# A fused attention and two-layer-pair kernel: GpSimd left out of the last two stages, operands loaded earlier

## The chip, the core and the metric

The kernel runs on one core of a Trainium2 chip, all of it in one launch. The metric is the time of one execution on the device in microseconds. The core's engines that matter here are TensorE (PE in the rows; its weight loads are PEld), VectorE (DVE), ScalarE (ACT), GpSimd (POOL) and SyncE (SP), which issues all DMA transfers of this kernel. Each works through its own instructions in order and waits for the others by semaphores.

## What is computed

Attention (local and coarse) over 4 x 8 heads of 576 tokens gives x of 2304 tokens by 512; two products, a gate, and two more products follow. Then comes the part that the change touches:

```python
def _moe_ref(x, w1, w2, w3, w_out):
    a = x @ w1
    b = x @ w2
    h = a * b @ w3
    return (h @ w_out).astype(np.float32)

def _moe2_ref(x, w_in, w_out):            # x: 2304 x 512, w_in: 512 x 2048, w_out: 2048 x 512
    h = x @ w_in
    g = h * (1.0 / (1.0 + np.exp(-h)))
    return (g @ w_out).astype(np.float32)
```

## The kernel before

**Precision.** An fp32 operand is held as two fp32r halves: a high part (a cast, mostly by ScalarE) and a low part, the operand less the high part (a subtraction by VectorE or GpSimd). Making the two is called a split below. A product takes three passes: high x high, low x high, high x low.

**Stages.** Up to about 459 us run attention and the first layer pair, whose result y goes to DRAM (`ydram`). The *hidden stage* makes g = silu(y @ w_in) and stores it in DRAM (`gd[i][t]`, four quadrants i). The *output stage* makes g @ w_out. Both use a 2 x 2 block scheme with 7 products in place of 8, so operands are sums and differences of quadrants.

**Hidden stage.** There are 3 token blocks t and 8 column pairs p, 24 units u = 8t + p (`h_unit`). A unit has 7 products, numbered 0 to 6 below, of 6 matmuls of 384 columns. They fall into four PSUM banks: hx gets products 0, 3 and 6, hy 1 and 5, hz 2, hv 4. ScalarE copies p1 (hx after 0), p5 (hy after 1), u (hx after 3) and v (hv after 4). TensorE can't go on adding to a bank before that copy, so product 3 needs p1, 5 needs p5, 6 needs u. VectorE's `keep` makes the four quadrants c by a sum of a bank and a copy (0 after product 2; 2 after product 5; 3 and 1 after product 6); ScalarE applies SiLU in place and SyncE stores it. There are 5 buffers c. `extra` holds functions that are put behind product i of a unit: splits of weights (`wc_high`/`wc_rest`, or `b_split` for the weights `wo` of the output stage), the load of the next token block's y, its four differences (`y_mix`) and 7 operand splits (`y_high`/`y_rest`).

**Output stage.** There are 9 sets n of 256 tokens (`o_set`), each with the products A11, A12, A22, S1, S2, S4, S3 (k = 0 to 6; the last set in another order), 24 matmuls of 256 columns each. Operands of set m = n + 1 are made in set n: `big` holds A22 and R, 2 loads; A11 and A12 one load each; S1 = R + A22 and S2 = S1 - A11 (`sums_12`, tile `tt_o`), S3 = A11 - R, S4 = A12 - S2 (`sum_34`, tiles `S3r`, `S4r`). Seven splits follow, four of their low parts on GpSimd. A11 and A12 share two rooms (tag `a`), so the next A11 can be loaded only when the product A11 is done. Results `co` are sums of a bank and a copy on VectorE, and are stored as 64 rows each.

**Order.** In these two stages the order on all five engines is the order in which the Python code issues (`tc.manual_schedule`); no planner moves anything. What stands first in the code stands first in each engine's queue.

## Time and profile before

| | us |
|---|---|
| median of 3 runs (870.33 to 873.45) | 870.39 |
| the profiled execution's own time | 877.89 |
| its span, first to last instruction | 876.1 |
| hidden stage, first product at | 459.05 |
| output stage, first product at | 649.12 |
| TensorE busy over the span | 825.7 (94%) |
| VectorE / ScalarE / GpSimd busy | 542.0 / 402.4 / 312.4 |

The times of stages come from the profiled execution, which took 0.9% more than the median of the runs. A stretch of time is read as "start : end" in us from the span's start. A wait in brackets behind an instruction is the idle time of its engine just ahead of it, with what ended it. TensorE's granted clock is 1.00 at 2.4 GHz and falls to half of that at 1.2 GHz.

### The profile page before, as it was taken

To read this page: it belongs to the slowest core of one execution; us is meant where nothing else is said; L and a number is where in the kernel's file an instruction comes from. 1 tells how busy PE (TensorE), PEld (TensorE's weight loads), DVE (VectorE), ACT (ScalarE), POOL (GpSimd) and SP (SyncE) were. 2 spreads that over 40 slices of the span, in tenths; PEclk is the share of its full clock that TensorE was granted. 3 is DMA by queue.
4 is the path that set the end of the run, shared out by engine and by line. 5 is a ranking of instruction groups with operands and counts; after the bars stand their busy time and mean duration, and the time that the engine had idled before them with its cause. 6 is when DMAs were issued, how large, how long until landed. Compare 5 with 4: busy or idle time off the path is not lost.

```text
span 876.1 us, 19413 instructions
## 1 busy us (share of the span) xinstructions
PE 825.7 (94%) x7774; PEld 766.7 (88%) x7774; DVE 542.0 (62%) x778; ACT 402.4 (46%) x1088; POOL 312.4 (36%) x218
## 2 busy tenths in 40 slices
PE   8999999999999999999999989989897898878897
PEld 4555799999999999999999989989897898878897
DVE  6988885764756563567733552253769665677662
ACT  6588664443444444323226664555664331333340
...
GB/s 304 370 178 244 228 162 173 118 203 121 185 145 195 174 102 148 50 282 223 143 143 246 113 107 141 137 95 192 292 238 123 115 120 120 96 77 87 106 118 43
DMA packets 101787, 141.44 MB, mean 161 GB/s; under 512 B 11584, under 2 KB 81216, under 8 KB 101696
## 3 DMA queue, kind: packets, MB, share of 16 engines
...
q8 instruction: 61, 1.00, 0.5%
...
## 4 chain that ended last, share of the span: by engine, by line
PE 67%; DVE 13%; DMA 10%; issue 5%; SPq 2%; ACT 2%; POOL 0%; DVEq 0%; ACTq 0%
PE ab L668 20%; PE y L736 12%; PE hx L1062 9%; DMA A<-gd 6%; PE hy L1062 5%; PE wp L624 5%; DVE tt_o L1041 4%; PE hv L1062 3%; DVE S4r L1041 3%; PE hz L1062 3%; PE ol L512 2%; DVE A L1041 2%; PE ox L1198 2%; DMA qk<-qk 1%; PE s L405 1%
## 5 line engine op out<-in xcount | busy, mean ns | idle before, releaser
L668 PE MATMUL ab<-x,w_wA 128*128 128x320 f32 (+1 forms) x768 | 107.1, 296 | 1.5 <-DVE w_wA L271 1.2
L736 PE MATMUL y<-c,w_wC 128*128 128x320 f32 (+1 forms) x768 | 107.0, 297 | 0.0
L668 PE MATMUL ab<-x,w_wB 128*128 128x320 f32 (+1 forms) x768 | 105.1, 295 | 0.0
L710 POOL TENSOR_TENSOR c<-cf,c 128x320 fp32r<-128x320 f32 (+1 forms) x64 | 70.0, 1094 | 98.4 <-DVE c L705 90.0
L668 PEld LDWEIGHTS ab<-x,w_wA 128*128 128x128 f32 x768 | 102.2, 188 | 2.4 <-DVE w_wA L271 1.5
L668 PEld LDWEIGHTS ab<-x,w_wB 128*128 128x128 f32 x768 | 101.6, 188 | 1.2 <-issue 0.4
L736 PEld LDWEIGHTS y<-c,w_wC 128*128 128x128 f32 x768 | 102.3, 188 | 0.3
L1053 ACT ACTIVATE c<-c 128x384 f32<-128x384 f32 x96 | 47.8, 522 | 67.1 <-DVE c L1041 65.0
L1062 PE MATMUL hx<-yc,wc 128*128 128x384 f32 x336 | 65.9, 338 | 6.9 <-ACT u L1074 4.6
L686 DVE TENSOR_TENSOR cf<-ab,af 128x320 f32<-128x320 f32 (+1 forms) x64 | 28.9, 452 | 63.2 <-PE ab L668 39.0
L1062 PEld LDWEIGHTS hx<-yc,wc 128*128 128x128 f32 x336 | 58.3, 188 | 9.7 <-ACT u L1074 7.2
L624 PE MATMUL wp<-w_wo,w_w 128*128 128x512 f32 x128 | 60.1, 602 | 0.2 <-DVE w_wo L194 0.2
L1198 PE MATMUL ox<-wo,A 128*128 128x256 f32 x216 | 37.8, 339 | 22.6 <-DVE A L1041 21.8
L680 ACT COPY af<-ab 128x320 f32<-128x320 f32 (+1 forms) x64 | 25.3, 397 | 73.1 <-PE ab L668 70.0
L474 POOL TENSOR_TENSOR vr<-vr 72x512 f32<-72x512 f32 x11 | 14.8, 1344 | 122.6 <-PE od L490 89.0
L1198 PEld LDWEIGHTS ox<-wo,A 128*128 128x128 f32 x216 | 35.0, 245 | 24.3 <-DVE A L1041 23.4
L1198 PE MATMUL oy<-wo,S 128*128 128x256 f32 x432 | 54.8, 283 | 0.5 <-ACT p5o L1208 0.5
L1198 PE MATMUL ox<-wo,S 128*128 128x256 f32 x432 | 53.9, 280 | 0.3 <-DVE S L1041 0.3
L1198 PEld LDWEIGHTS oy<-wo,S 128*128 128x128 f32 x432 | 53.0, 190 | 0.7 <-ACT p5o L1208 0.7
L1198 PEld LDWEIGHTS ox<-wo,S 128*128 128x128 f32 x432 | 52.0, 189 | 0.6 <-DVE S L1041 0.5
L1062 PE MATMUL hy<-yc,wc 128*128 128x384 f32 x240 | 48.8, 338 | 0.0
L330 ACT ACTIVATE band<-band,sml 128x38 f32<-128x38 f32 x144 | 44.9, 318 | 4.4 <-DVE sml L421 4.4
...
## 6 DMA issues: line engine op xcount, KB each, us to landing
...
```

The costliest lines, as they stand in the source:

```text
L330: nc.scalar.activation(E[:, j, :], src[j], AF.Exp, bias=z[:, j:j + 1], scale=scale, accum_out=z[:, NQB + j:NQB + j + 1],)
L512: nc.tensor.matmul(acc[h][r, c0:c0 + QW], lhsT=v[k, sub, c, r], rhs=ET[k, c, q0:q0 + QW], start=True, stop=True,)
L624: nc.tensor.matmul(wp_ps[half, j], lhsT=w3v[:, k, j * P:(j + 1) * P], rhs=wov[:, k, :], start=(gp == 0 and k == 0), stop=(gp == 3 and k == 1),
L668: nc.tensor.matmul(acc[:, :N], lhsT=wv[:, i, w, kk, :], rhs=X[b, h, kk][:, j, :], start=(n == 0), stop=(n == 11),)
L680: mark(nc.scalar.copy(af, C.pop(("ab", b, h, m, 0))[:, :N]))
L686: nc.vector.tensor_tensor(out=cf, in0=C.pop(("ab", b, h, m, 1))[:, :N], in1=C.pop(("af", b, h, m)), op=ALU.mult)
L710: mark(nc.gpsimd.tensor_tensor(out=c[:, 1], in0=C.pop(("cf", b, h, m)), in1=c[:, 0].bitcast(F32), op=ALU.subtract))
L736: nc.tensor.matmul(acc[:, :N], lhsT=WP[kf // 2][:, i, kf % 2, ec * P:(ec + 1) * P], rhs=c[:, j, :], start=(kf == 0 and n == 0), stop=(kf = ...
L1041: (e or nc.vector).tensor_tensor(out=out_, in0=in0, in1=in1, op=op_)
L1053: nc.scalar.activation(v, v, AF.Silu)
L1062: nc.tensor.matmul(acc, lhsT=WC[s][:, a, c, kt * P:(kt + 1) * P], rhs=y[:, b, kt, :], start=(n == 0 and i in (0, 1, 2, 4)), stop=(n == 5), ...
L1198: nc.tensor.matmul(acc, lhsT=A[:, a, p * P:(p + 1) * P], rhs=B_[name, p // 4][:, b, p % 4, :], start=(p == 0 and q == 0 and name in begin) ...
```

## The change

In the hidden stage and the output stage every GpSimd instruction moves to VectorE (`y_mix` from the second token block on, all low parts). SiLU and its store no longer follow `keep` at once: they go to a list `late`, and `catch_up` issues them behind later copies (quadrant 0 behind copy v, 2 behind the next unit's p1, 3 and 1 behind its p5). Splits stand behind products 1, 3 and 5. The y operands 2 and 3 of the second block get the two rooms of A11 and A12 (tag `a`), which stand empty until the output stage; for the third block operands 4 and 5 get the room `cx`. The first set's loads come a unit or more earlier. In the output stage a table `PLAN` says behind which product each step stands. A11 is loaded twice, once into its own room and once into the room of S3, from which S3 and S2 are made; A12 likewise a second time into the room of S4. `big` is loaded two sets ahead in place of one, and a product's loads are issued ahead of its results.

VectorE in the output stage, from S3's sum of set 4 to the end of its preparation; `tt_o` holds S1 and S2, `big` A22 and R, `co` are results. Before:

```order
L1041 TENSOR_TENSOR S3r4_9117<-A11_4_9034,big4_9003 128x1024
L1041 TENSOR_TENSOR tt_o4_9122<-big4_9003 128x1024
L1041 TENSOR_TENSOR tt_o4_9122<-tt_o4_9122,A11_4_9034 128x1024
L1041 TENSOR_TENSOR A11_4_9034<-A11_4_9034 128x1024
L1041 TENSOR_TENSOR S4r4_9152<-A12_4_9064,tt_o4_9122 128x1024
L1041 TENSOR_TENSOR co1_3_9180<-oy3_8998,u2o3_9001 128x256
L1041 TENSOR_TENSOR A12_4_9064<-A12_4_9064 128x1024
L1041 TENSOR_TENSOR co3_3_9210<-ox3_8996,p5o3_9002 128x256
L1041 TENSOR_TENSOR co2_3_9214<-ox3_8996,cov_3_9090 128x256
L1041 TENSOR_TENSOR S2_4_9221<-tt_o4_9122,S2_4_9221 128x1024
```

And now, from S4's sum of set 3 on:

```order
L1046 TENSOR_TENSOR S4r3_9040<-S4_3_8960,tt_o3_8870 128x1024
L1046 TENSOR_TENSOR S4_3_8960<-S4r3_9040,S4_3_8960 128x1024
L1046 TENSOR_TENSOR co0_3_9070<-oz3_9005,p1o3_9008 128x256
L1046 TENSOR_TENSOR tt_o4_9100<-big4_8899 128x1024
L1046 TENSOR_TENSOR tt_o4_9100<-tt_o4_9100,S3_4_9037 128x1024
L1046 TENSOR_TENSOR A11_4_9035<-A11_4_9035 128x1024
L1046 TENSOR_TENSOR S3r4_9133<-S3_4_9037,big4_8899 128x1024
L1046 TENSOR_TENSOR A12_4_9068<-A12_4_9068 128x1024
L1046 TENSOR_TENSOR S3_4_9037<-S3r4_9133,S3_4_9037 128x1024
L1046 TENSOR_TENSOR big4_8899<-big4_8899 128x1024
L1046 TENSOR_TENSOR co1_3_9192<-oy3_9006,u2o3_9009 128x256
L1046 TENSOR_TENSOR S1_4_9196<-tt_o4_9100,S1_4_9196 128x1024
```

S4 has moved behind the set's own start, S3 is read from its second copy, the low parts of S3, A22 (`big`), S1 and S4, GpSimd's before, stand in the row, and the sums begin before the first split instead of all standing together.

SyncE in the output stage, one set's loads from `gd` and the stores to `out`. Before:

```order
L1112 DMA big4_9003<-gd3_1_91 128x8x128
L1112 DMA big4_9003<-gd2_1_88 128x8x128
L1112 DMA A11_4_9034<-gd0_1_82 128x8x128
L1034 DMA out<-co0_3_9060 64x256
L1035 DMA out<-co0_3_9060 64x256
L1112 DMA A12_4_9064<-gd1_1_85 128x8x128
L1034 DMA out<-co1_3_9180 64x256
L1035 DMA out<-co1_3_9180 64x256
L1034 DMA out<-co3_3_9210 64x256
L1035 DMA out<-co3_3_9210 64x256
L1034 DMA out<-co2_3_9214 64x256
```

And now:

```order
L1133 DMA A11_4_9035<-gd0_1_82 128x8x128
L1133 DMA S3_4_9037<-gd0_1_82 128x8x128
L1133 DMA A12_4_9068<-gd1_1_85 128x8x128
L1039 DMA out<-co0_3_9070 64x256
L1040 DMA out<-co0_3_9070 64x256
L1133 DMA big5_9129<-gd3_1_91 128x8x128
L1133 DMA big5_9129<-gd2_1_88 128x8x128
L1133 DMA S4_4_9190<-gd1_1_85 128x8x128
L1039 DMA out<-co1_3_9192 64x256
L1040 DMA out<-co1_3_9192 64x256
L1039 DMA out<-co3_3_9223 64x256
```

There are six loads where there were four, `big` is that of set 5 and no longer of set 4, and each load stands ahead of the stores of the same product.

ScalarE in unit 7, the last one of token block 0, up to p1 of unit 8; `yc` and `cx` are operand splits, ACTIVATE is SiLU. Before:

```order
L1068 COPY p17_6985<-hx7_6981 128x384
L1070 COPY p57_6987<-hy7_6983 128x384
L930 CAST yc1_2_7003<-yr1_6604 128x768
L1053 ACTIVATE c0_7_7012<-c0_7_7012 128x384
L1074 COPY u27_6986<-hx7_6981 128x384
L930 CAST yc1_4_7026<-tt1_6681 128x768
L1076 COPY v47_6988<-hv7_6984 128x384
L1053 ACTIVATE c2_7_7045<-c2_7_7045 128x384
L930 CAST yc1_6_7049<-yr1_6604 128x768
L1053 ACTIVATE c3_7_7058<-c3_7_7058 128x384
L1053 ACTIVATE c1_7_7062<-c1_7_7062 128x384
L1068 COPY p18_7070<-hx8_7066 128x384
```

And now:

```order
L1084 COPY p17_6985<-hx7_6981 128x384
L1062 ACTIVATE c2_6_6966<-c2_6_6966 128x384
L1087 COPY p57_6987<-hy7_6983 128x384
L1062 ACTIVATE c3_6_6977<-c3_6_6977 128x384
L1062 ACTIVATE c1_6_6979<-c1_6_6979 128x384
L935 CAST yc1_4_7009<-tt1_6648 128x768
L1092 COPY u27_6986<-hx7_6981 128x384
L935 CAST yc1_5_7027<-yr1_6598 128x768
L1094 COPY v47_6988<-hv7_6984 128x384
L1062 ACTIVATE c0_7_7018<-c0_7_7018 128x384
L935 CAST yc1_6_7047<-yr1_6598 128x768
L1084 COPY p18_7064<-hx8_7060 128x384
```

The SiLUs of quadrants 2, 3 and 1 are those of unit 6 (`c2_6`), and no SiLU of unit 7's late sums stands ahead of p1 of unit 8.

The diff, cut:

```diff
@@ -917,13 +917,18 @@
                 "p (i k n) -> p i k n", i=3, k=2
             )
         b[out_] = b["b12"] if i == 2 else b["tt"][:, (0, 1, None, 2)[i]]
-        nc.gpsimd.tensor_tensor(out=b[out_], in0=b[in0], in1=b[in1], op=ALU.subtract)
+        (nc.vector if t else nc.gpsimd).tensor_tensor(
+            out=b[out_], in0=b[in0], in1=b[in1], op=ALU.subtract
+        )
 
     def y_high(t, i, e=None):
-        if (t == 1 and i < 2) or (t == 2 and 2 <= i < 4):
+        if i // 2 == 2 * t - 2 and t:
             if t not in CX:
                 CX[t] = b2[0].tile([P, 8 * NH], F32, tag="cx", name=f"cx{t}", bufs=1)
             d = CX[t].bitcast(F32R).rearrange("p (i l k n) -> p i l k n", i=2, l=2, k=2)[:, i % 2]
+        elif t == 1 and 2 <= i < 4:
+            d = b2[0].tile([P, 2, 8 * P], F32R, tag="a", name=f"yc{t}_{i}", bufs=2)
+            d = d[:, :, :2 * NH].rearrange("p l (k n) -> p l k n", k=2)
         else:
             d = yp[0].tile([P, 2, 2, NH], F32R, tag="c_", name=f"yc{t}_{i}", bufs=7)
         if e is None:
@@ -1040,6 +1045,8 @@
     def tt(out_, in0, in1, op_=ALU.add, e=None):
         (e or nc.vector).tensor_tensor(out=out_, in0=in0, in1=in1, op=op_)
 
+    late = []
+
     def h_unit(u, extra):
         t, p = divmod(u, 8)
         X_, Z_, Y_ = mm_tile(f"hx{u}"), t_tile(f"hz{u}"), s_tile(f"hy{u}")
@@ -1050,8 +1057,17 @@
         def keep(i, src, add):
             v = temp("c", f"{i}_{u}", bufs=5)
             tt(v, src, add)
-            nc.scalar.activation(v, v, AF.Silu)
-            nc.sync.dma_start(gd[i][t][:, p, :], v)
+
+            def silu():
+                nc.scalar.activation(v, v, AF.Silu)
+                nc.sync.dma_start(gd[i][t][:, p, :], v)
+
+            late.append(silu)
+
+        def catch_up(n):
+            for fn in late[:n]:
+                fn()
+            del late[:n]
 
         for i, (name, o) in enumerate(CH):
             acc = (X_, Y_, Z_, X_, V_, Y_, X_)[i]
@@ -1066,14 +1082,17 @@
                     n += 1
             if i == 0:
                 nc.scalar.copy(p1, X_)
+                catch_up(1)
             elif i == 1:
                 nc.scalar.copy(p5, Y_)
+                catch_up(2)
             elif i == 2:
                 keep(0, Z_, p1)
             elif i == 3:
                 nc.scalar.copy(u2, X_)
             elif i == 4:
                 nc.scalar.copy(v4, V_)
+                catch_up(1)
             elif i == 5:
                 keep(2, Y_, u2)
             else:
@@ -1081,6 +1100,8 @@
                 keep(1, X_, v4)
             for fn in extra.get(i, ()):
                 fn()
+        if u == NUN - 1:
+            catch_up(3)
 
 
 
...
@@ -1128,7 +1149,7 @@
 
     def a_fetch(n, name):
         a_tile(n, name)
-        fetch(n, int(name != "A11"), plain(n, name))
+        fetch(n, int(name in ("A12", "S4")), plain(n, name))
 
     def big_fetch(n):
         home, tag = (b2[0], "cx") if n % 2 else (yp[1], "raw")
@@ -1138,31 +1159,28 @@
         fetch(n, 3, plain(n, "A22"))
         fetch(n, 2, R_[n])
 
...
     o_, T_ = [], {}
 
-    def sums_12(n):
+    def sums_12(n, a11):
         both = yp[1].tile([P, 6 * NH], F32, tag="tt", name=f"tt_o{n}")
         T_[n, "S1"], T_[n, "S2"] = both[:, :CHUNK], both[:, CHUNK:2 * CHUNK]
         tt(T_[n, "S1"], R_[n], plain(n, "A22"))
-        tt(T_[n, "S2"], T_[n, "S1"], plain(n, "A11"), ALU.subtract)
+        tt(T_[n, "S2"], T_[n, "S1"], a11, ALU.subtract)
 
...
         if n == 0:
             a_fetch(0, "S4")
-            s_split(0, "S1", nc.gpsimd)
-            s_split(0, "S2", nc.vector)
-        if n + 1 < NSET:
-            big_fetch(n + 1)
+            s_split(0, "S1")
+            b_split(11)
+            s_split(0, "S2")
+            big_fetch(1)
         for k, name in enumerate(order):
             acc, A = bank[name], A_.pop((n, name))
             for p in range(8):
@@ -1200,6 +1218,7 @@
                         start=(p == 0 and q == 0 and name in begin), stop=(p == 7 and q == 2),
                         skip_group_check=True,
                     )
+            take(n, k, True)
             if name == "A11":
                 nc.scalar.copy(p1, X_)
             elif name == "A12":
@@ -1222,40 +1241,63 @@
...
-            if n == 0:
-                if k == 0:
-                    s_split(0, "S3", nc.vector)
-                    b_split(10)
-                elif k == 1:
-                    b_split(11)
-                    sum_34(0, "S4", plain(0, "S4"), T_[0, "S2"])
-                    s_split(0, "S4", nc.vector)
-                elif k == 2:
-                    b_split(12)
-                elif k == 3:
-                    b_split(13)
-            elif k == 0:
-                s_split(n, "S4", nc.gpsimd)
-            m = n + 1
-            if last:
-                continue
-            if k == 0:
-                a_fetch(m, "A11")
-            elif k == 1:
-                a_fetch(m, "A12")
-            if k == (3 if n else 4):
-                sum_34(m, "S3", plain(m, "A11"), R_[m])
-                s_split(m, "S3", nc.gpsimd)
-                sums_12(m)
-            if k == (4 if n else 5):
-                a_split(m, "A11", nc.vector)
-                sum_34(m, "S4", plain(m, "A12"), T_[m, "S2"])
-                a_split(m, "A22", nc.gpsimd)
-            if k == 5:
-                a_split(m, "A12", nc.vector)
-            if k == 6:
-                s_split(m, "S1", nc.gpsimd)
-                s_split(m, "S2", nc.vector)
+            take(n, k, False)
+
+    def take(n, k, loads):
+        for step in PLAN[min(n, 2)].get(k, ()):
+            who, _, what = step.partition(" ")
+            m = n + int(who == "next")
+            if m < NSET and loads == (what in LOADS):
+                steps[what](m)
+
+    LOADS = ("f11", "f12", "f4", "big")
+    steps = {
...
+        "big": lambda m: big_fetch(m + 1) if m + 1 < NSET else None,
+        "f11": lambda m: (a_fetch(m, "A11"), a_fetch(m, "S3")),
+        "f12": lambda m: a_fetch(m, "A12"),
+        "f4": lambda m: a_fetch(m, "S4"),
+        "sum12": lambda m: sums_12(m, plain(m, "S3")),
+        "sum3": lambda m: sum_34(m, "S3", plain(m, "S3"), R_[m]),
+        "sum4": lambda m: sum_34(m, "S4", plain(m, "S4"), T_[m, "S2"]),
...
+    }
+    PLAN = (
+        {
+            0: ("this s3", "next f11"),
+            1: ("this sum4", "this s4", "next f12"),
+            2: ("this b12",),
+            3: ("this b13", "next a11", "next big"),
+            4: ("next a12", "next sum12"),
+            5: ("next sum3", "next a22", "next f4"),
+            6: ("next s1",),
+        },
+        {
+            0: ("this s2", "next f11"),
+            1: ("this s3", "this sum4", "this s4", "next f12"),
+            2: ("next sum12", "next a11"),
+            3: ("next sum3", "next a12", "next big"),
+            4: ("next s3", "next a22"),
+            5: ("next s1", "next f4"),
+            6: ("next s2",),
+        },
+        {
+            0: ("this sum4", "this s4", "next f11"),
+            1: ("next f12",),
+            2: ("next sum12", "next a11"),
+            3: ("next sum3", "next a12", "next big"),
+            4: ("next s3", "next a22"),
+            5: ("next s1", "next f4"),
+            6: ("next s2",),
+        },
+    )
 
     E = mybir.EngineType
     with tc.manual_schedule(engines={E.PE, E.DVE, E.Activation, E.Pool, E.SP}):
@@ -1271,36 +1313,29 @@
             if t == 0:
                 todo = {0: (4, 5), 1: (6,), 2: (7, 8), 3: (9, 10), 4: (11, 12), 5: (13,)}
                 for k, s in enumerate(todo.get(p, ())):
-                    put((0, 3)[k], lambda s=s: wc_high(s), lambda s=s: wc_rest(s))
+                    put((1, 3)[k], lambda s=s: wc_high(s), lambda s=s: wc_rest(s, nc.vector))
             if t + 1 < NT:
                 if p == 1:
                     put(6, lambda t=t: y_load(t + 1))
                 if 2 <= p < 6:
-                    put(6, lambda t=t, p=p: y_mix(t + 1, p - 2))
-                if p == 6:
-                    for i in range(2):
-                        put((0, 3)[i], lambda t=t, i=i: y_high(t + 1, i),
-                            lambda t=t, i=i: y_rest(t + 1, i))
-                if p == 7:
-                    for i in range(2, 7):
-                        put(i - 1, lambda t=t, i=i: y_high(t + 1, i, nc.vector if i % 2 else None),
-                            lambda t=t, i=i: y_rest(t + 1, i))
+                    put(3, lambda t=t, p=p: y_mix(t + 1, p - 2))
+                todo = {5: ((4, 0),), 6: ((1, 1), (3, 2), (5, 3)), 7: ((1, 4), (3, 5), (5, 6))}
+                for k, i in todo.get(p, ()):
+                    put(k, lambda t=t, i=i: y_high(t + 1, i),
+                        lambda t=t, i=i: y_rest(t + 1, i, nc.vector))
             else:
                 loads = {1: (0, 1), 2: (2, 3, 4), 3: (5, 6), 4: (7,), 5: (8, 9), 6: (10, 11), 7: (12, 13)}
-                splits = {3: (0, 1), 4: (2, 3), 5: (4, 5), 6: (6, 7), 7: (8, 9)}
+                splits = {3: (0, 1), 4: (2, 3), 5: (4, 5), 6: (6, 7), 7: (8, 9, 10)}
+                if p == 0:
+                    put(0, lambda: big_fetch(0))
+                    put(0, lambda: a_fetch(0, "A11"), lambda: a_fetch(0, "A12"))
                 if p == 1:
-                    put(6, lambda: big_fetch(0))
+                    put(3, lambda: sums_12(0, plain(0, "A11")))
+                    put(5, lambda: sum_34(0, "S3", plain(0, "A11"), R_[0]))
                 if p == 2:
-                    put(3, lambda: a_fetch(0, "A11"))
-                if p == 3:
-                    put(3, lambda: a_fetch(0, "A12"))
-                    put(6, lambda: sums_12(0))
-                if p == 4:
-                    put(2, lambda: sum_34(0, "S3", plain(0, "A11"), R_[0]))
-                if 4 <= p < 7:
-                    name = ("A11", "A22", "A12")[p - 4]
-                    put(5, lambda name=name: a_split(0, name, nc.gpsimd, cast=nc.vector))
-                for k, i in zip(splits.get(p, ()), (0, 3)):
+                    for k, name in ((1, "A11"), (3, "A22"), (5, "A12")):
+                        put(k, lambda name=name: a_split(0, name))
+                for k, i in zip(splits.get(p, ()), (1, 3, 5)):
                     put(i, lambda k=k: b_split(k))
                 for k in loads.get(p, ()):
                     put(6, lambda k=k: b_load(k))
```

## Rows read from the trace of the kernel before

**Rows 1.** Busy time by stretch (us, count): PE, PEld, DVE, ACT, POOL; granted clock, DMA, GB/s.
```profile
649.12:872.95 223.83, 193.29 (x1513) 189.23 (x1512) 148.58 (x99) 75.08 (x103) 103.69 (x36) 0.95 0.41 106
459.05:649.12 190.07, 180.91 (x1010) 177.71 (x1009) 87.53 (x120) 110.92 (x221) 59.50 (x29) 0.98 0.52 170
```

**Rows 2.** Timeline of PE in undisturbed stretches: start us, duration us, instruction.
```profile
465.32 2.24 PE L1062 MATMUL hx<-yc,wc 128*128 128x384 f32 x12
472.60 2.24 PE L1062 MATMUL hx<-yc,wc 128*128 128x384 f32 x12
...
686.51 3.04 PE L1198 MATMUL oy<-wo,S 128*128 128x256 f32 x24
...
689.39 3.05 PE L1198 MATMUL ox<-wo,S 128*128 128x256 f32 x24
```

**Rows 3.** Waits of PE in the last two stages: us in total, times, longest.
```profile
PE ox L1198 <- DVE A L1041: 21.8, 8, 3.5
PE oz L1198 <- DVE A L1041: 7.2, 7, 1.7
PE hx L1062 <- ACT u L1074: 4.6, 8, 0.8
PE hx L1062 <- ACT p L1068: 4.6, 2, 2.3
```

**Rows 4.** Timeline between the second and third output set; idle time ahead in brackets.
```profile
685.04 1.20 SPq L1112 DMA_DIRECT2D A<-gd  x1
...
691.75 1.23 DVE L1041 TENSOR_TENSOR S3r<-A,big 128x1024 f32<-128x1024 f32 x1 [6.92 <-DMA A<-gd]
...
694.13 2.41 POOL L1041 TENSOR_TENSOR S<-S3r,S 128x1024 fp32r<-128x1024 f32 x1 [10.73 <-DVE tt_o L1041]
694.14 3.48 DVE L1041 TENSOR_TENSOR tt_o<-tt_o,A 128x1024 f32<-128x1024 f32 x1
...
697.73 3.20 DVE L1041 TENSOR_TENSOR A<-A 128x1024 fp32r<-128x1024 f32 x1
...
700.99 2.98 PE L1198 MATMUL ox<-wo,A 128*128 128x256 f32 x23 [2.81 <-DVE A L1041]
...
704.53 1.21 DVE L1041 TENSOR_TENSOR A<-A 128x1024 fp32r<-128x1024 f32 x1
```

**Rows 5.** Timeline of PE after its longest wait in the output stage.
```profile
674.24 5.28 PE L1198 MATMUL ox<-wo,A 128*128 128x256 f32 x23 [3.22 <-DVE A L1041]
```

**Rows 6.** Timeline of the hidden stage: end of token block 0; unit 19.
```profile
518.02 1.21 PE L1062 MATMUL hx<-yc,wc 128*128 128x384 f32 x6
...
524.65 1.32 PE L1062 MATMUL hx<-yc,wc 128*128 128x384 f32 x6 [2.25 <-ACT p L1068]
...
529.46 0.87 PE L1062 MATMUL hx<-yc,wc 128*128 128x384 f32 x4
...
612.04 1.23 DVE L950 TENSOR_TENSOR wo<-wo 128x1024 fp32r<-128x1024 f32 x1 [3.23 <-ACT wo L947]
...
613.18 0.55 DVE L1041 TENSOR_TENSOR c<-hz,p 128x384 f32<-128x384 f32 x1
...
613.77 0.52 ACT L1053 ACTIVATE c<-c 128x384 f32<-128x384 f32 x1 [1.38 <-DVE c L1041]
614.20 0.46 ACT L1074 COPY u<-hx 128x384 f32<-128x384 f32 x1
...
614.71 2.35 PE L1062 MATMUL hx<-yc,wc 128*128 128x384 f32 x12 [0.71 <-ACT u L1074]
```

**Rows 7.** Groups by form in the two stages: busy us, mean ns of one, idle before.
```profile
L1041 DVE TENSOR_TENSOR A<-A 128x1024 fp32r<-128x1024 f32 x16 | 37.1, 2320 | 0.8
...
L1145 ACT CAST A<-A 128x1024 fp32r<-128x1024 f32 x16 | 16.8, 1049 | 0.0
...
L938 DVE TENSOR_TENSOR yc<-yr,yc 128x768 fp32r<-128x768 f32 x2 | 1.9, 958 | 0.1
```

**Rows 8.** The stretch of one set's three loads: length, granted clock, DMA, GB/s.
```profile
683.65:692.00 8.35, 1.00 0.97 251
```

24 lines of the change are left out of this document (15 added, 9 removed).

## The prediction

> **What bounds the kernel now.** I read the stage windows first, then TensorE's waits, then the timeline at the places that the waits name. The last two stages start with the first hidden-layer product at 459.05 us and the first output product at 649.12 us, so they are windows of 190.07 us and 223.83 us, and TensorE's record is busy for 180.91 and 193.29 us of them [rows 1]. To see what the products need when nothing holds them, I take their distance in an undisturbed stretch. A hidden unit (7 products of 6 matmuls) starts 7.28 us after the one before it (465.32 and 472.60), and one of the seven products of an output set starts 2.88 us after the one before it (686.51 and 689.39) [rows 2]. So 24 units need 24 x 7.28 = 174.7 us and 9 sets need 9 x 7 x 2.88 = 181.4 us. The excess is 15.4 us in the hidden stage and 42.4 us in the output stage, 57.8 us in all: the most that any change around these products can give.
>
> Who makes TensorE late: in the output stage VectorE's low parts of A11 (21.8 us, 8 times) and A12 (7.2 us, 7 times); in the hidden stage ScalarE's copies u (4.6 us, 8 times) and p1 (4.6 us, twice) [rows 3]. These waits add up to 38.2 us, and the rest of the 57.8 us is mostly the clock: after the longest wait 23 matmuls of A11 took 5.28 us where the undisturbed product takes 2.88 [rows 5], and the granted clock averages 0.95 and 0.98 in the two windows, 1.00 being 2.4 GHz [rows 1].
>
> **Why A11 is late in a set.** SyncE issues the load of the next A11 at 685.04; VectorE stands idle 6.92 us for it and begins S3 at 691.75; then everything is due at once. S2's sum takes 3.48 us beside a GpSimd subtraction of 2.41 us that began 0.01 us earlier, A11's low part 3.20, yet A12's low part, with GpSimd idle, takes 1.21 us for the same 1024 columns [rows 4]. A11 is ready at 700.9, TensorE having waited 2.81 us. Two causes, then: a late load, and VectorE operations that stretch while GpSimd works on SBUF.
>
> The Trainium skill (SBUF — State Buffer, § Who interferes with whom) says that a VectorE instruction with two SBUF inputs contends with a GpSimd instruction that reads SBUF and that the later one waits for the whole of the other. By that rule, 2.41 + about 1.2 us gives the 3.48 us, and the trace agrees.
>
> **The change, part by part.**
>
> (1) *Output stage, work.* GpSimd's four splits a set go to VectorE, which then has 7 low parts, 4 sums and 4 results of 256 columns. With GpSimd silent I price the 11 large ones at 1.21 us (the unstretched row) [rows 4] and the results at no more than 0.55, a sum of 384 columns [rows 6]: 13.3 + 2.2 = 15.5 us of 20.2. ScalarE has 7 casts of 1.05 us [rows 7] and 4 copies of at most 0.46, again the wider one [rows 6]: 9.2 us. Neither is the bound.
>
> (2) *Output stage, order.* I walk one set from its start, products ending at 2.9, 5.8, 8.6, 11.5, 14.4, 17.3, 20.2. The loads of A11 and of its copy in S3's tile are issued at 2.9. Before, 1.57 MB (A22, R, A11) issued from 683.65 on were there at 691.75, in 8.1 us; that window, start-up and all, moved 251 GB/s [rows 4, 8]. So 1.05 MB should land by 9 to 11. S1 and S2's sums end near 10.5, A11's low part at 11.5 to 12.5, S3's sum at 13, A12's low part at 14.5, those of S3 and A22 at 18.5, S1 at 20, S2 at 22.5. TensorE wants A11 at 20.2, A12 at 23, A22 at 26, S1 at 29, S2 at 32. The smallest margin is 7.5 us, so all 29.0 us of waits on A11 and A12 go, and with them the half-clock stretches that follow. What is late next in a set: S4, whose operand is loaded at 17.3 and split at about 6 of the next set, wanted at 14.4. SyncE's queue is cleared for this by putting each load ahead of the result stores of the same product; those wait for VectorE, and nobody waits for them.
>
> (3) *Set 0* has no such lead. After the last unit VectorE and ScalarE must do S1, half of a weight, S2, S3 and S4; with casts of 1.05 and low parts of 1.21 in line, S4's low part ends 14 to 15 us after TensorE begins the set, and is wanted at 14.4. I charge 0 to 1 us, and take 0.5.
>
> (4) *Hidden stage, unit ends.* TensorE's product 6 needs the copy u. Before, VectorE waited 3.23 us for a cast, did the weight's low part, only then the sum that SiLU (613.77) needed, and the copy u stood behind that SiLU; TensorE waited 0.71 us at 614.71 [rows 6]. Now each SiLU stands two products later, and a split behind product 1, 3 or 5. What remains is a loop over the engines, from one unit's first cast to the next one's: cast 1.05, two low parts 2.42, y sum 0.96, four sums 2.2, last SiLU 0.52 = 7.2 us in units 2 to 5; with three weights or operands (units 18 and 23) 1.05 + 3.63 + 2.2 + 0.52 = 7.4 [rows 4, 6, 7]. TensorE's unit is 7.28. This is a close race, though instructions of one engine overlap a little (613.18 + 0.55 against the next start). I charge the hidden stage 3 us for these units and for stores that now stand behind weight loads in SyncE's queue. The bounds are 0 and the 7 us that the short stalls cost today (15.4 less the two below).
>
> (5) *Hidden stage, change of token block.* At unit 8 (and 16) TensorE waited 2.25 us for p1, behind ScalarE's casts of y operands [rows 6]; with slow matmuls behind it the unit took 529.46 − 518.02 = 11.4 us, 4.2 above 7.28. That is 8.4 us for two. Now operands 0 to 3 are split in units 5 to 7 into rooms of their own (two of them in A11's and A12's), and 4 to 6 behind the products of unit 7 that free theirs, with over two units' slack for the first and seven products for the last. ScalarE's 4 copies, 4 SiLUs and 3 casts of unit 7 are 1.8 + 2.1 + 3.2 = 7.1 us even at the 1024-column cast's 1.05 (these casts have 768), so p1 of unit 8 doesn't queue. Both stalls should go; a remainder is in the 3 us.
>
> (6) *Everything before 459 us* keeps its instructions; I cost it at nothing.
>
> Sum: 57.8 − 3 − 0.5 − 0.5 (small waits between sets) = 53.8 us off the profiled execution of 877.89 us. It ran 0.9% above the median 870.39, so I scale by 0.9915: 53.3 us, and **817 us**. With no residue at all it is 870.4 − 57.3 = 813; with twice the residue, 821.
>
> **Rivals.**
>
> *The loop in the hidden stage is the new bound.* If the race in (4) is lost by 0.3 to 0.6 us in most of the 14 units that carry splits, and the unit ends stay as long as today, the stage keeps its 15.4 us: 817 + 12.3 = 829. For it: ScalarE, by the same sum, at 7.1 us of 7.28 in units 18 and 23. Against: the loops of the other units come to 7.2 or less, and the overlap works for it.
>
> *Transfers pace the sets.* A set now moves six loads of 0.52 MB and 0.52 MB of results, 3.67 MB. At 251 GB/s that is 14.6 us of 20.2 [rows 8]. At the hidden stage's mean of 170 GB/s [rows 1] it is 21.6 us, 1.4 more a set, 13 in all: 830. Against: that mean holds idle time.
>
> *The clock gives nothing back.* If only TensorE's idle time came back, 223.83 − 193.29 + 190.07 − 180.91 = 39.7 us [rows 1], less 4, the time would be 870.4 − 35.4 = 835. For that the matmuls would have to stay slow with no wait ahead of them, which [rows 2] speaks against. The Trainium skill (Perfetto Trace Analysis, § Identifying the Most-Contended Engine) calls matmul busy time a bad measure of the distance to the limit; by that rule the 39.7 is too small, and the product distances agree.
>
> *VectorE becomes the bound: slower.* If its operations are long for another reason than GpSimd (ScalarE's casts, the loads), they keep today's mean: 2.32 us for A's low parts [rows 7]. Then a set costs 11 x 2.32 + 2.2 = 27.7 us, nine cost 249.5 against 223.8 before, and with 12 us saved in the hidden stage: 870 + 26 − 12 = 884. It decides from 1.6 us an operation on ((20.2 − 2.2) / 11); the kernel is slower than before from 2.2. Against it: 1.21 us at 704.53 [rows 4].
>
> That the change doesn't do what it says is excluded: no GpSimd instruction is left behind the last of the stage before 459 us.
>
> **Chances.** Forecast 817 (813 to 821): 0.64. Hidden-stage loop, 829: 0.17. Transfers, 830 and up: 0.08, a quarter of it so far up that no change can be told. Clock, 835: 0.05. VectorE bound: 0.06. Leaving out the last and the far ends, the range is 811 to 832. A measurement of this kernel tells about 0.5% from no change: faster 0.92, same 0.02, slower 0.06.
>
> **What would show it.** Right: output products 2.9 us apart over all nine sets, no wait on A11 or A12, granted clock 1.00 in both windows, VectorE's 1024-column operations near 1.2 us throughout, some 182 us from the first output product to the last one's end, units 8 and 16 of 7.3 us. Wrong: a wait of product 6 on u that grows through units 2 to 5 (loop); VectorE waiting for a load in every set, with A11 ready after 20 us (transfers); slow VectorE rows without GpSimd.

## The result, and the profile after

The changed kernel takes **819.87 us** (median of 4 runs, 815.67 to 821.88), beside 871.81 us for the kernel before on the same chip: a ratio of 0.9397, 95% interval 0.9353 to 0.9442. The forecast was 817.0 in a range of 811 to 832. The profiled execution took 821.88 us, with a span of 819.9; the one of before took 877.89.

Windows of the output stage and the hidden stage (length, busy time and count of PE, PEld, DVE, ACT, POOL, granted clock, DMA share, GB/s), to be held against [rows 1], and TensorE's waits in the two stages, against [rows 3]:

```profile
637.15:816.74 179.59, 178.35 (x1513) 177.43 (x1512) 127.42 (x136) 75.94 (x102) 0.00 (x0) 1.00 0.69 180
460.48:637.15 176.67, 175.56 (x1010) 174.92 (x1009) 96.10 (x141) 117.13 (x229) 0.00 (x0) 1.00 0.56 182
```

```profile
PE hx L1078 <- ACT u L1092: 1.0, 1, 1.0
PE ov L1216 <- DVE big L1046: 0.9, 1, 0.9
PE ox L1216 <- ACT u2o L1229: 0.4, 1, 0.4
```

The hidden stage fell from 190.07 to 176.67 us, the output stage from 223.83 to 179.59: 57.6 us, of which the first stage, 1.4 us longer in this execution, takes a little back. TensorE is busy for 99% of both windows at a granted clock of 1.00, that is at 2.4 GHz, and its waits in the two stages, 38.2 us before, are down to 2.3. No wait on A11 or A12 is left.

One set of the output stage: PE's timeline from a set's start to the next set's (start us, duration us), and VectorE's steps for the next A11 and A12 in it, against [rows 4]:

```profile
698.88 2.88 PE L1216 MATMUL ox<-wo,A 128*128 128x256 f32 x24
701.60 2.88 PE L1216 MATMUL oz<-wo,A 128*128 128x256 f32 x24
704.32 2.88 PE L1216 MATMUL ov<-wo,big 128*128 128x256 f32 x24
707.04 3.04 PE L1216 MATMUL oy<-wo,S 128*128 128x256 f32 x24
709.92 3.04 PE L1216 MATMUL ox<-wo,S 128*128 128x256 f32 x24
...
718.42 2.88 PE L1216 MATMUL ox<-wo,A 128*128 128x256 f32 x24
```

```profile
708.38 1.22 DVE L1046 TENSOR_TENSOR tt_o<-tt_o,S 128x1024 f32<-128x1024 f32 x1 [2.31 <-DMA S<-gd]
709.52 1.22 DVE L1046 TENSOR_TENSOR A<-A 128x1024 fp32r<-128x1024 f32 x1
...
712.65 1.23 DVE L1046 TENSOR_TENSOR A<-A 128x1024 fp32r<-128x1024 f32 x1 [0.77 <-ACT A L1165]
```

The sum S2 still stands idle for a load, 2.31 us, but A11's low part is done at 710.74, 7.7 us before the product that needs it starts at 718.42. In [rows 4] TensorE had been waiting for it for 2.81 us.

VectorE by form in the output stage (count | busy us, mean ns of one | idle before), against [rows 7]:

```profile
L1046 DVE TENSOR_TENSOR A<-A 128x1024 fp32r<-128x1024 f32 x16 | 19.5, 1220 | 4.8 <-ACT A L1165 4.8
...
L1046 DVE TENSOR_TENSOR tt_o<-tt_o,S 128x1024 f32<-128x1024 f32 x8 | 9.8, 1224 | 15.1 <-DMA S<-gd 15.0
```

The low parts of A take 1220 ns where they took 2320. The question left open by the result is which part of the change brought what, since GpSimd's silence, the order, the loads and the late SiLU came together.

### The profile page after: what moved, and what is told of

It reads as the page before. It is cut to its first block, busy times and chain, and to the rows that moved or that the text cites. A ratio compares the mean times of both kernels' runs of the same rounds, so it can differ in the third digit from the quotient of the medians.

```text
span 819.9 us, 19334 instructions
## 1 busy us (share of the span) xinstructions
PE 806.0 (98%) x7774; PEld 751.9 (92%) x7774; DVE 525.5 (64%) x835; ACT 408.9 (50%) x1095; POOL 148.9 (18%) x154
## 4 chain that ended last, share of the span: by engine, by line
PE 85%; DMA 7%; DVE 5%; issue 1%; SPq 1%; ACT 1%; POOL 0%; DVEq 0%; ACTq 0%
PE ab L668 21%; PE y L736 13%; PE hx L1078 8%; PE ox L1216 8%; PE wp L624 6%; PE hy L1078 5%; PE oy L1216 5%; PE oz L1216 3%; PE hv L1078 3%; PE hz L1078 3%; PE ov L1216 2%; PE ol L512 2%; DMA gd<-c 2%; DMA A<-gd 2%; DMA qk<-qk 1%
## 5 line engine op out<-in xcount | busy, mean ns | idle before, releaser
L1078 PE MATMUL hx<-yc,wc 128*128 128x384 f32 x384 | 74.8, 335 | 1.1 <-ACT u L1092 1.0
L1078 PEld LDWEIGHTS hx<-yc,wc 128*128 128x128 f32 x384 | 67.2, 188 | 1.7 <-ACT u L1092 1.7
L624 PE MATMUL wp<-w_wo,w_w 128*128 128x512 f32 x128 | 62.1, 619 | 0.2 <-DVE w_wo L194 0.2
L1216 PE MATMUL ox<-wo,S 128*128 128x256 f32 x432 | 53.8, 281 | 0.4 <-ACT u2o L1229 0.4
L624 PEld LDWEIGHTS wp<-w_wo,w_w 128*128 128x128 f32 x128 | 23.2, 196 | 22.5 <-issue 20.2
L1078 PE MATMUL hy<-yc,wc 128*128 128x384 f32 x192 | 38.4, 334 | 0.0
L747 ACT COPY yo<-y 128x320 f32<-128x320 f32 (+1 forms) x32 | 12.6, 396 | 51.8 <-PE y L736 40.9
```

The costliest lines, as they stand in the source:

```text
L624: nc.tensor.matmul(wp_ps[half, j], lhsT=w3v[:, k, j * P:(j + 1) * P], rhs=wov[:, k, :], start=(gp == 0 and k == 0), stop=(gp == 3 and k == 1),
L1078: nc.tensor.matmul(acc, lhsT=WC[s][:, a, c, kt * P:(kt + 1) * P], rhs=y[:, b, kt, :], start=(n == 0 and i in (0, 1, 2, 4)), stop=(n == 5), ...
L1216: nc.tensor.matmul(acc, lhsT=A[:, a, p * P:(p + 1) * P], rhs=B_[name, p // 4][:, b, p % 4, :], start=(p == 0 and q == 0 and name in begin) ...
```

## Experiments

All but x10 are edits of the changed kernel; x10 is an edit of the kernel before. Stage times are the windows of the profiled execution, from the stage's first product on.

### The output stage: GpSimd or the order?

**x1** gives GpSimd four low parts of a set back and keeps order and loads.

```diff
-        tt(d[:, 1], src, d[:, 0].bitcast(F32), ALU.subtract)
+        e = nc.gpsimd if n and name in ("S1", "A22", "S3", "S4") else None
+        tt(d[:, 1], src, d[:, 0].bitcast(F32), ALU.subtract, e)
```

> The changed kernel with one thing undone: in the output stage GpSimd makes the low parts of S1, A22, S3 and S4 of sets 1 to 8 again. Loads and order stay new. Theory (the early loads and the spread order give the margin): VectorE has 7 large operations left, and four GpSimd operations of 2.4 us lengthen at most as many of them, so a set's work is about 10.7 + 9.6 = 20.3 us, just a set; output stage 180 to 190 us (179.6 in the changed kernel), total 820 to 830. Rival (GpSimd's absence is what removed the waits): the waits on A11 and A12 come back with 1 to 3 us each, output stage 200 to 220 us, total 840 to 865.

**x2** is the reverse: order and loads of before, all low parts on VectorE.

```diff
-            big_fetch(1)
+        if n + 1 < NSET:
+            big_fetch(n + 1)
...
-            take(n, k, True)
...
+            take(n, k, True)
...
-        "f11": lambda m: (a_fetch(m, "A11"), a_fetch(m, "S3")),
+        "f11": lambda m: a_fetch(m, "A11"),
...
+    OLD = {
+        0: ("this s4", "next f11"),
+        1: ("next f12",),
+        3: ("next sum3", "next s3", "next sum12"),
+        4: ("next a11", "next sum4", "next a22"),
+        5: ("next a12",),
+        6: ("next s1", "next s2"),
+    }
```

> The changed kernel with the output stage's order and loads of before (A11 and A12 loaded once, behind the result stores; all sums of the next set together behind product 3; A22 and R one set ahead), but with VectorE making all low parts. So GpSimd left out alone. Theory (both causes count): VectorE begins S3's sum where it did, some 6 us before A11 is wanted; with S3's low part in line it has five operations of 1.2 us and a wait for a cast ahead of A11, so A11 and A12 are each about 1 us late: output stage 188 to 202 us, total 828 to 842. Rival 1 (GpSimd alone): 180 us, 820. Rival 2 (the late load alone): 212 us or more, 852 or more.

Measured: x1 820.68 us (0.9366 of before, 0.9304 to 0.9429), x2 843.18 (0.9610, 0.9543 to 0.9676). The output stage's window of x1 and two of VectorE's groups in it:

```profile
634.55:815.62 181.07, 178.40 (x1513) 177.19 (x1512) 114.57 (x104) 75.83 (x102) 83.60 (x32) 1.00 0.67 179
```

```profile
L1046 DVE TENSOR_TENSOR S<-tt_o,S 128x1024 fp32r<-128x1024 f32 x10 | 26.7, 2674 | 2.3 <-ACT S L1165 2.3
L1046 DVE TENSOR_TENSOR A<-A 128x1024 fp32r<-128x1024 f32 x16 | 19.5, 1218 | 4.9 <-ACT A L1165 4.9
```

The same of x2, with TensorE's waits and two rows of its timeline between two sets:

```profile
639.31:839.04 199.73, 184.80 (x1513) 181.35 (x1512) 126.79 (x136) 74.80 (x102) 0.00 (x0) 0.99 0.46 120
```

```profile
PE ox L1217 <- DVE A L1046: 10.1, 8, 3.7
PE oz L1217 <- DVE A L1046: 4.8, 7, 0.7
```

```profile
699.79 1.23 DVE L1046 TENSOR_TENSOR S3r<-A,big 128x1024 f32<-128x1024 f32 x1 [6.43 <-DMA A<-gd]
...
707.14 2.88 PE L1217 MATMUL ox<-wo,A 128*128 128x256 f32 x23 [0.78 <-DVE A L1046]
```

In x1 GpSimd is busy for 83.6 us and VectorE's low parts of S1 and S2 are stretched to 2674 ns on average, but A's low parts keep their 1218 ns: in the new order they stand where GpSimd has nothing to do. The stage takes 181.07 us. TensorE waits 2.6 us in it, all in set 1 (1.3 of them for GpSimd's own low parts) and none for A11 or A12. So the new order is enough with GpSimd at work; that a stretched A11 would do no harm in it, x1 doesn't show. In x2 VectorE is quick, stands idle 6.43 us for the load as in [rows 4] and is late by 0.78 us instead of 2.81. So this table holds for the output stage:

| output stage, us | order and loads of before | order and loads of after |
|---|---|---|
| GpSimd takes part | 223.83 | 181.07 |
| GpSimd left out | 199.73 | 179.59 |

Either part alone helps, the order by 42.8 us and GpSimd's silence by 24.1, but the second adds only 1.5 to the first, and the medians of x1 and the changed kernel (820.68 and 819.87) don't tell even that. x2's time came out 1 us above its range; nothing hangs on that.

### The hidden stage: five kernels

**x9** gives GpSimd back its work there (the y differences and every second low part of weights and y operands):

```diff
-        (nc.vector if t else nc.gpsimd).tensor_tensor(
+        nc.gpsimd.tensor_tensor(
...
-        for fn in halves(B_[OPS[i], h], nc.vector):
+        for fn in halves(B_[OPS[i], h], nc.gpsimd if h else nc.vector):
```

> The changed kernel with GpSimd back in the hidden stage alone: the y differences of blocks 1 and 2, every second low part of weights and of y operands. SiLU late, positions and rooms stay new. Theory (in this stage the late SiLU and the places count, not GpSimd): the loop from cast to SiLU gets shorter by a low part on VectorE and longer where a VectorE operation meets one of GpSimd; a few waits of 0.2 to 1 us: hidden stage 176 to 180 us, total 819 to 824. Rival (GpSimd's absence counts here too): 184 us or more, total 827 or more.

**x4** splits the y operands behind the products of before, in the rooms of before:

```diff
-        if i // 2 == 2 * t - 2 and t:
+        if (t == 1 and i < 2) or (t == 2 and 2 <= i < 4):
...
-                todo = {5: ((4, 0),), 6: ((1, 1), (3, 2), (5, 3)), 7: ((1, 4), (3, 5), (5, 6))}
+                todo = {6: ((0, 0), (3, 1)), 7: ((1, 2), (2, 3), (3, 4), (4, 5), (5, 6))}
```

> The changed kernel with the y operands split where they were before (two in unit 6, five in unit 7 and 15, in the rooms of before), by ScalarE and VectorE; SiLU stays late. Theory (unit 7's queue is what made p1 of unit 8 late): ScalarE has 5 casts of 0.84 us beside 4 copies and 4 SiLUs, 8.1 us for a unit of 7.28, and the operands whose room is freed last come last; p1 is 0.5 to 2 us late at units 8 and 16, with slow matmuls behind it: hidden stage 179 to 184 us, total 822 to 827. Rival (the late SiLU alone frees p1): 177 us, 820.

**x3** issues SiLU and its store at once:

```diff
-            late.append(silu)
+            silu()
```

> The changed kernel with SiLU and its store issued right behind the sum, as before; positions of the splits, rooms and the output stage stay new. Theory (the copy u stands behind a SiLU that waits for a sum behind a split): product 6 waits 0.5 to 1.0 us for u in the units that have a split behind product 1, about 14 of 24: hidden stage 184 to 191 us (176.7 in the changed kernel), total 827 to 834. Rival (positions and VectorE's shorter operations did it): 177 to 179 us, 820 to 822.

**x13** joins x3 and x4. What is left of the change in this stage is VectorE in GpSimd's place, and also three shifts that the expectation doesn't name: the y differences stand behind product 3 where they stood behind 6, a weight's first split behind product 1 where it stood behind 0, and set 0's loads, sums and splits come earlier:

> The changed kernel with SiLU at once and the y operands split at the places of before, so that in the hidden stage what is left of the change is VectorE in GpSimd's place. Theory (with SiLU at once the places of the splits decide how late p1 is; GpSimd's absence does nothing): hidden stage 187 to 193 us as before, output stage 180, 829 to 836 us. Rival (VectorE's added work makes the sums late wherever the splits stand): 200 to 212 us, 842 to 856.

**x10** is the kernel before with `late`, `catch_up` and their calls, and nothing else:

> The kernel before with one edit, the late SiLU of the changed kernel: GpSimd, loads, order and rooms stay. Theory (the late SiLU alone brings the hidden stage to its undisturbed 7.28 us a unit): hidden stage 177 to 179 us, output stage as before near 224, 858 to 862 us in all. Rival (it does so only with GpSimd off VectorE's sums): hidden stage 183 to 190, 865 to 873 us.

Measured: x9 820.25 us (0.9375, 0.9323 to 0.9426), x4 816.88 (0.9325, 0.9273 to 0.9378), x3 856.03 (0.9783, 0.9724 to 0.9841), x13 858.57 (0.9825, 0.9789 to 0.9862), x10 863.56 (0.9896, 0.9857 to 0.9935). Windows of the hidden stage, in the order x9, x4, x3, x13, x10, one fence each:

```profile
460.47:637.24 176.77, 175.30 (x1011) 174.89 (x1009) 74.69 (x116) 116.62 (x229) 52.32 (x26) 1.00 0.57 182
```

```profile
455.86:633.61 177.75, 175.95 (x1011) 174.83 (x1009) 96.21 (x141) 116.58 (x229) 0.00 (x0) 1.00 0.57 181
```

```profile
460.36:671.88 211.52, 189.41 (x1010) 180.88 (x1009) 96.49 (x141) 117.02 (x228) 0.00 (x0) 0.96 0.48 152
```

```profile
457.77:669.68 211.91, 189.88 (x1010) 182.53 (x1009) 97.04 (x141) 116.88 (x228) 0.00 (x0) 0.95 0.48 152
```

```profile
458.61:635.37 176.76, 175.43 (x1010) 174.88 (x1009) 88.91 (x120) 109.78 (x222) 64.25 (x29) 1.00 0.56 182
```

| hidden stage, us | SiLU at once | SiLU late |
|---|---|---|
| GpSimd takes part | 190.07 (before) | 176.76 (x10), 176.77 (x9) |
| GpSimd left out | 211.91 (x13), 211.52 (x3) | 177.75 (x4), 176.67 (after) |

The column decides. By these windows the late SiLU alone brings the whole 13.4 us (x4: 12.3), whoever subtracts and wherever the y operands are split. By the medians x10 gains 10.4 us (873.99 to 863.56; 5.7 to 12.5 by the interval) and stays 1.6 us above its range; the window of before is that of one execution, and a long one. With SiLU at once, the rest of the change costs 22 us in this stage. That this is GpSimd's absence is not shown, since x13 keeps the three shifts named above and no run has GpSimd back with SiLU at once. I had expected 7 to 14 us of x3, 2 to 7 of x4 and, of x13, at first the stage of before; that of x3 foresaw the waits for u (they came to 4.2 us) and not those for p1 (17.4), and those of x4 and x13 took the places of the y operands' splits for the cause. But x4, with the old places, takes only 1.1 us more than the changed kernel, and x13, with the old places, is as slow as x3. The Trainium skill (Perfetto Trace Analysis, § Optimizing GPSIMD Operations) advises "Prefer implementations on other engines where possible." In this stage the runs show no gain by it with SiLU late (176.76 and 176.77 us with GpSimd, 176.67 without), and with SiLU at once a loss in which its part is not separated.

How the time is lost is best seen in x13 at its longest wait. A stretch of its timeline:

```profile
557.26 0.96 DVE L920 TENSOR_TENSOR tt<-yr 128x768 f32<-128x768 f32 x1 [8.43 <-DMA gd<-c]
558.14 0.55 DVE L1046 TENSOR_TENSOR c<-hy,u 128x384 f32<-128x384 f32 x1
...
558.73 1.45 ACT L1062 ACTIVATE c<-c 128x384 f32<-128x384 f32 x3 [7.88 <-DVE c L1046]
...
560.08 0.46 ACT L1084 COPY p<-hx 128x384 f32<-128x384 f32 x1
...
560.60 2.29 PE L1078 MATMUL hx<-yc,wc 128*128 128x384 f32 x6 [5.12 <-ACT p L1084]
```

Four engines stand in a row here. The first difference of the next block's y reads a tile that is still being loaded, and VectorE stands 8.43 us for it (the profile names the store next to those loads in SyncE's queue; that it is the load is my reading of the operand). The quadrant sums stand behind it, ScalarE's SiLU waits 7.88 us for a sum, the copy p1 stands behind the SiLU, and TensorE waits 5.12 us for p1. The same instruction in x10, where GpSimd does it, and in the changed kernel:

```profile
541.41 1.86 POOL L920 TENSOR_TENSOR tt<-yr 128x768 f32<-128x768 f32 x1 [20.06 <-DMA gd<-c]
```

```profile
542.65 0.96 DVE L920 TENSOR_TENSOR tt<-yr 128x768 f32<-128x768 f32 x1 [5.31 <-DMA gd<-c]
```

On GpSimd, there behind product 6, it may stand for 20.06 us, because nothing that TensorE needs soon is queued behind it. On VectorE it stands 5.31 us in the changed kernel too, and TensorE doesn't notice: the sums behind it are late as well, but their SiLUs no longer stand ahead of p1. Behind product 6, as before, it would have stood after the three sums that SiLU waits for here; that place was not tried on VectorE. A load has a part in this chain and in one of 1.79 us. In the next longest waits of x13 (3.03, 3.03 and 2.88 us) the sums stand behind low parts that wait for ScalarE's casts, as at unit 8:

```profile
529.01 0.96 DVE L943 TENSOR_TENSOR yc<-yr,yc 128x768 fp32r<-128x768 f32 x1 [1.31 <-ACT yc L935]
...
531.92 2.29 PE L1078 MATMUL hx<-yc,wc 128*128 128x384 f32 x6 [3.03 <-ACT p L1084]
```

All such chains together make 21.6 us of waits in x13, and the matmuls behind them run at the lower clock (mean granted clock 0.95), which adds 14 us of busy time (189.88 against 175.56):

```profile
PE hx L1078 <- ACT p L1084: 17.0, 7, 5.1
PE hx L1078 <- ACT u L1092: 4.6, 10, 0.6
```

### A silent GpSimd, the traffic and the copies

**x5** lets GpSimd subtract in a tile of its own, 16 times 512 columns a set, beside the changed kernel:

```diff
+                nc.gpsimd.tensor_tensor(out=own[:, :256], in0=own[:, :256], in1=p1, op=ALU.subtract)
+                for _ in range(16):
+                    nc.gpsimd.tensor_tensor(out=own, in0=own, in1=own, op=ALU.subtract)
```

> The changed kernel with work of GpSimd's own in the output stage: in each set one subtraction of 256 columns behind p1 and 16 of 512 columns on a tile that nobody else reads, some 19 us of a set. Nothing of the computation depends on it. Theory (VectorE's operations with two SBUF operands wait for GpSimd's operation under way): the two engines alternate, VectorE's 1024-column operations take 2 to 3.5 us, a set costs about 15.5 + 16 to 19 = 30 to 35 us, output stage 260 to 310 us, total 900 to 950. Rival (the stretching of before came from the tiles both worked on, or from ScalarE and the loads): VectorE's operations stay at 1.22 us and the total at 820.

Measured in one run: 895.55 us (before: 872.76). Its output stage, VectorE's group of A's low parts, and TensorE's largest wait:

```profile
636.72:872.11 235.39, 193.42 (x1513) 189.54 (x1512) 187.87 (x136) 74.76 (x102) 218.91 (x135) 0.91 0.53 137
```

```profile
L1046 DVE TENSOR_TENSOR A<-A 128x1024 fp32r<-128x1024 f32 x16 | 32.6, 2038 | 0.0
```

```profile
PE ox L1216 <- ACT p1o L1223: 28.1, 4, 12.0
```

The same low part takes 2038 ns in place of 1220, though GpSimd shares no data with it: this is the stretch that the prediction put down to GpSimd. The Trainium skill (SBUF — State Buffer, § Who interferes with whom) has it that a VectorE instruction with two SBUF inputs and a GpSimd instruction that reads SBUF shut each other out; the trace agrees. The size of the loss proves less. 28.1 us are waits for p1o, whose room GpSimd still had to read behind its 16 subtractions, so part of the 56 us is the experiment's own making, and my 260 to 310 was too high.

**x6** adds four loads of 256 KB a set into a tile that nobody reads; **x11** moves the same bytes at the same places from memory to memory, into ground that no later transfer waits for:

```diff
+            if n + 1 < NSET and k in (2, 4):
+                for half in range(2):
+                    nc.sync.dma_start(
+                        own.rearrange("p (k n) -> p k n", k=4),
+                        gd[2][(n + 1) // 3][:, 4 * half:4 * half + 4, :P],
+                    )
```

and in x11, with r counted on from call to call:

```diff
-                        own.rearrange("p (k n) -> p k n", k=4),
+                        wsd[:, r:r + 2, :].rearrange("p a (k n) -> p (a k) n", k=2),
```

> The changed kernel with 1.05 MB more of loads in each of the first eight output sets (four loads of 256 KB behind products 2 and 4, into a tile that nobody reads). A set then moves 4.7 MB, 234 GB/s at 20.2 us, where the changed kernel moves 180 in the output stage. Theory (transfers have room): S2's sum and A11 come later by up to 4 us, less than their margin; output stage 180 to 184 us, total 820 to 825. Rival (transfers nearly pace the sets): sets of 22 us and more, output stage 195 us or more, total 835 or more.

> The changed kernel with four more transfers of 256 KB a set, in the places of x6, but from memory to memory, so that none waits for a room: 4.7 MB a set as there. Theory (x6 lost its 26 us because SyncE's queue stood for the one room that its own loads shared, 73.3 us by the queue's waits): output stage 179 to 185 us, 817 to 824 us in all. Rival (the transfers themselves pace a set at that size): 195 to 206 us, 833 to 845.

Measured: x6 845.20 us (0.9683, 0.9646 to 0.9720), x11 818.21 (0.9374, 0.9344 to 0.9404). x6's output stage and the largest wait of SyncE's queue in it, then x11's output stage:

```profile
637.81:843.65 205.84, 186.20 (x1513) 183.17 (x1512) 126.76 (x136) 75.37 (x102) 0.00 (x0) 0.98 0.72 198
```

```profile
SPq L1224 <- DMA own<-gd: 73.3, 24, 5.5
```

```profile
632.06:811.90 179.84, 178.10 (x1513) 177.13 (x1512) 127.41 (x136) 76.18 (x102) 0.00 (x0) 1.00 0.83 227
```

x6 came out 20 us above what I had expected and seemed to show that transfers pace the sets. They don't: its four loads shared one room, each stood in the queue until the one before had landed, 73.3 us in all, and the kernel's own loads stood behind them. With the same traffic and no such wait x11 moves 227 GB/s at 0.83 of the DMA engines and loses nothing. Its added bytes end in memory, though, and not in the core as those of x6; loads into the core without the wait were not tried.

**x7** loads A11 and A12 once, and puts the sums that read them ahead of the splits:

```diff
-        "f11": lambda m: (a_fetch(m, "A11"), a_fetch(m, "S3")),
+        "f11": lambda m: a_fetch(m, "A11"),
...
-            2: ("next sum12", "next a11"),
-            3: ("next sum3", "next a12", "next big"),
-            4: ("next s3", "next a22"),
-            5: ("next s1", "next f4"),
+            2: ("next sum12", "next sum3", "next a11"),
+            3: ("next s3", "next sum4", "next big"),
+            4: ("next a12", "next a22"),
+            5: ("next s1", "next s4"),
```

> The changed kernel with A11 and A12 loaded once: S2's and S3's sums read A11's own room ahead of its split, S4's sum A12's; splits of S3 and S4 a product earlier. A set moves 2.6 MB. Theory (the lead in time carries it, the second copies only free the order): A11 is still ready 4 us or more ahead of its turn; output stage 178 to 182 us, total 817 to 823. Rival (the second copies are needed, since the sums hold up the splits): waits on A11 or A12 of 0.5 us and more in each set, output stage 185 us or more, total 826 or more.

**x12** is x7 with set 0's loads spread. The reason is the one wait left in the hidden stage of the changed kernel, at the end of unit 17. Two rows of SyncE's queue and four of the timeline there:

```profile
579.81 1.32 SPq L1133 DMA_DIRECT2D big<-gd  x2
581.22 2.76 SPq L1133 DMA_DIRECT2D A<-gd  x2
...
590.35 0.56 DVE L1046 TENSOR_TENSOR c<-hx,v 128x384 f32<-128x384 f32 x1 [5.14 <-DMA gd<-c]
...
590.94 0.52 ACT L1062 ACTIVATE c<-c 128x384 f32<-128x384 f32 x1 [3.26 <-DVE c L1046]
591.37 0.46 ACT L1092 COPY u<-hx 128x384 f32<-128x384 f32 x1
...
591.89 1.33 PE L1078 MATMUL hx<-yc,wc 128*128 128x384 f32 x6 [1.03 <-ACT u L1092]
```

Four loads of 0.52 MB are issued in one go; the stores of c stand behind them, and VectorE stands 5.14 us for a buffer c. The SiLU of that sum, quadrant 1 of unit 16, stands ahead of the copy u of unit 17, and product 6 waits 1.03 us for u.

```diff
-                    put(0, lambda: a_fetch(0, "A11"), lambda: a_fetch(0, "A12"))
+                    put(4, lambda: a_fetch(0, "A11"))
+                if p == 1:
+                    put(1, lambda: a_fetch(0, "A12"))
```

> The kernel of x7 (A11 and A12 loaded once) with the first loads of set 0 spread over units 16 and 17 instead of standing behind one another at the start of unit 16. Theory (the 1.0 us wait of unit 17 came from a store behind those loads): no wait in unit 17, hidden stage 175.5 to 176, 813 to 816 us. Rival (another wait is late next, or the runs' spread hides it): 815 to 818, not to be told from x7.

Measured: x7 815.96 us (0.9338, 0.9306 to 0.9371), x12 815.44 (0.9332, 0.9304 to 0.9359). The two stages of x7, then of x12:

```profile
454.89:631.32 176.43, 175.31 (x1010) 174.86 (x1009) 96.30 (x141) 117.01 (x229) 0.00 (x0) 1.00 0.57 182
631.32:810.73 179.41, 177.96 (x1513) 177.29 (x1512) 127.63 (x136) 75.11 (x102) 0.00 (x0) 1.00 0.51 134
```

```profile
454.89:630.53 175.64, 175.46 (x1011) 174.85 (x1009) 96.22 (x141) 117.10 (x229) 0.00 (x0) 1.00 0.57 183
630.53:809.59 179.06, 177.86 (x1513) 177.25 (x1512) 127.70 (x136) 75.14 (x102) 0.00 (x0) 1.00 0.51 134
```

The second copies aren't needed: 134 GB/s do. The wait of unit 17 is gone in x12 (what is left in the stage is one of 0.2 us, in unit 20), and its two stages together take 354.7 us where the changed kernel takes 356.3. x7's two stages take 355.8, so that its gain in them is 0.4. Both are the shortest kernels here by median, some 4 us below the changed one, yet the intervals of the ratios overlap, the part before the hidden stage was 5.6 us shorter in their profiled executions, and x12 can't be told from x7.

## Why the prediction was right

The time lay in the range because the main steps held. Two causes in it, of (3) and (5), were wrong though their sizes fitted, and two sizes of the sum were off in opposite directions; that 817 came so near is in part luck.

- **(1) Work.** Held. The 1.21 us taken from the one unstretched row became 1.22 for all 1024-column operations; VectorE is busy 127.42 / 9 = 14.2 us a set where 15.5 were forecast, ScalarE 8.4 where 9.2 were.
- **(2) Order.** Held almost to the row: A11 ready 11.9 us after the set's start (forecast 11.5 to 12.5), A12 15.0 (14.5), the load waited for until 9.5 (9 to 11). x1 and x2 add that the step rests on the order and the loads; GpSimd's silence isn't needed for it, since A's low parts take 1218 ns in the new order with GpSimd at work too.
- **(3) Set 0.** S4 wasn't late. In its stead A22's low part of set 1 was, by 0.9 us. The charge of 0.5 us was near the size by luck, for another reason.
- **(4) Unit ends.** Right in size (176.67 against 174.7 undisturbed, 2.0 us where 3 were charged), wrong in its loop: units 18 and 23, which came to 7.4 us by the sum, show no wait, and the only one is that of unit 17, from stores behind loads in SyncE's queue; the same step had named such stores, behind weight loads where these were set 0's. The sum took the loop for closed. The late SiLU opens it: a SiLU ahead of a copy now belongs to a sum of two products earlier, and only where VectorE stands as long as the 5.14 us in unit 17 does the copy come late. The late SiLU wasn't one of several things that help, it is the whole gain of the stage (x10).
- **(5) Token blocks.** The size held: unit 8 takes 7.4 us in the changed kernel, from its first product to unit 9's (the fence below). The cause didn't. x4 has the old places and rooms, x10 the old places, rooms and engines, and neither has that wait, so it is enough to take the SiLUs from ahead of p1; the new places and rooms weren't needed.

```profile
518.75 1.21 PE L1078 MATMUL hx<-cx,wc 128*128 128x384 f32 x6
...
526.12 1.20 PE L1078 MATMUL hx<-cx,wc 128*128 128x384 f32 x6
```

- **(6) The part before.** Its instructions were the same, as said, but its length varied by 7.6 us between executions (last section), more than the whole residue of the sum.
- **What the working lacked.** The load of y that VectorE now waits for, 5.31 us, was in no term. It cost nothing with SiLU late; with SiLU at once it is behind the longest wait of x13, 5.12 us.
- **The sum.** In the profiled executions the two stages gave 57.6 us where 53.8 were forecast. The undisturbed set was mis-sized: I took 2.88 us for each product from two S products [rows 2], but in the set shown above the next product starts 2.72 us after A11, A12 and A22, so a set takes 718.42 − 698.88 = 19.5 us and not 20.2. Nine of those are 175.9 us, 5.5 less than the 181.4 forecast; the stage took 179.59, so its residue was 3.7 us where I had charged 1 (3.1 of it in sets 0 to 2). By the medians the gain is smaller, 51.9 us where 53.3 were forecast, since the profiled execution of before lay 6.1 us above its median and that of the changed kernel 2.0; the scale of 0.9915 took only 0.5 us off for that. Nor was 870.39 a firm base: the kernel before had medians from 870.4 to 874.4 in the series run here, 871.81 in that of the result. So 817.0 was 2.9 us short, 1.4 by the base and 1.4 by the gain.
- **The rivals.** The hidden loop as bound, 829: not so while SiLU is late, and the side on which this kernel is weakest, since x3 shows it with one line undone. Transfers: fallen, by x11 at 1.05 MB a set more. Clock: fallen, 1.00 in both windows. VectorE bound: fallen with 1.22 us, though x5 shows VectorE with 187.87 / 9 = 20.9 us of work a set, more than the 19.5 of TensorE's set, once GpSimd is busy nearly all the time.
